# A block-sorted attention with a bilinear feed-forward: one engine-model ordering of all work, Strassen products for three batches, and q and v of two batches by DMA

## The chip, the cores and the metric

The kernel runs on one core of one Trainium2 chip. The metric is the device time of one execution in microseconds (us). Before and after run in turn on the same chip. A profile is taken of one of the runs; its span, from the first to the last instruction, is about 1 to 2 us shorter than the time.

Engines are named as the profile names them: PE (TensorE, matmuls), PEld (its weight loads), DVE (VectorE), ACT (ScalarE), POOL (GpSimd), SP (SyncE, which only issues DMAs here).

## The reference

```python
# q, k, v: (4, 8, 768, 64); sort_net: (4, 8, 8, 8)
P = sort_net
for _ in range(5):                                   # Sinkhorn
    P = exp(P - max(P, -1)); P = P / sum(P, -1); P = P / sum(P, -2)
k_sorted = einsum('bhij,bhjcd->bhicd', P, k_blocks)  # 8 blocks of 96 tokens
v_sorted = einsum('bhij,bhjcd->bhicd', P, v_blocks)
attn = softmax(scale * q_b @ k_sb^T) @ v_sb          # inside each block
x = attn, heads side by side                         # (3072, 512)
out = ((x @ w_a) * (x @ w_b)) @ w_out                # w_a, w_b: 512 x 1536
```

There are four batches of 768 tokens. The feed-forward part has by far the most arithmetic: per batch, the two products with `w_a` and `w_b` ("a, b products") are 48 groups of four matmuls, and the product with `w_out` ("output stage") is six groups of twelve.

## The kernel before

The order of the PE instructions is written by hand: the attention of the next batch is dealt out, unit by unit, between the a, b products of this one.

```python
tc.tile_pool(name="psA", bufs=2, space=PSUM) as psA   # attention: [P, 2, 512] tiles
tc.tile_pool(name="psB", bufs=1, space=PSUM) as psB   # transposes
tc.tile_pool(name="psF", bufs=3, space=PSUM) as psF   # products: [P, 512] tiles, one bank

def ffn_a(b, m, t, pool):
    pf = ffn_mm(b, m, t, w_a_sb, pool)        # four matmuls of 128 x 384 into a psF tile
    a_sb = ffp.tile([P, HW], BF16, tag="a_sb", bufs=4)
    nc.scalar.copy(out=a_sb, in_=pf[:, 0:HW])
def ffn_b(b, m, t, pool):
    pf = ffn_mm(b, m, t, w_b_sb, pool)
    nc.vector.tensor_tensor(out=hT..., in0=a_sb..., in1=pf..., op=ALU.mult)
def ffn_out(b, t, c, pool):
    po = pool.tile([P, DMODEL], FP32, tag="F")
    for m in range(KO):                       # twelve matmuls of 128 x 512
        nc.tensor.matmul(po, lhsT=hT[:, m, c0:c0 + P], rhs=w_out_sb[:, m, :], ...)
    copy(nc.scalar if c % 2 == 0 else nc.vector, o_sb, po)
    ... # two DMA stores
... # (attention: transposes of q and v on PE, mixing of k and v on PE, scores, exp, products, transposes)
```

The softmax here doesn't subtract the row's maximum and nothing guards it: scores larger than these inputs give would overflow.

## Time and profile before

The profile's span is 259.0 us.

First the page: a line with each engine's busy time, the busy tenths of PE and the clock granted to it in 40 slices of the span, and the chain of waits that ended last, by engine and by line.

```profile
PE 247.8 (96%) x2406; PEld 146.9 (57%) x2415; DVE 126.7 (49%) x293; ACT 98.2 (38%) x191; POOL 50.9 (20%) x71
...
PE   6978999999999999999999999999999999999992
...
PEclk9999999999999999999999999999999999999999
...
PE 88%; DVE 2%; POOL 2%; ACT 2%; DMA 2%; issue 1%; POOLq 0%; ACTq 0%
```

PE is busy in every slice after the start, at full clock, and 88% of the chain is PE. So time can only be taken out by taking work off PE, or by shortening the start (first a, b product at 27.25 us).

### The profile page before, as it was taken

What the parts mean: (1) busy time and instruction counts of PE and PEld (TensorE: products, weight loads), DVE (VectorE), ACT (ScalarE), POOL (GpSimd) and SP (SyncE); (2) the same over time, 40 slices, a digit from 0 to 9 for tenths busy, and PEclk for the clock granted to TensorE, in tenths of its full rate; (3) what the DMA queues carried; (4) which work ended last, traced back from release to release, by engine and by line L of the source; (5) the groups of instructions that cost most, each with busy time, mean ns of one, the idle gap of its engine ahead of it and who ended that gap; (6) DMA issues with size and microseconds to landing.
All of it is one profiled execution on the core that took longest, in us unless ns stands there. A gap on an engine that the chain in (4) does not pass through costs nothing.

```text
span 259.0 us, 5786 instructions
## 1 busy us (share of the span) xinstructions
PE 247.8 (96%) x2406; PEld 146.9 (57%) x2415; DVE 126.7 (49%) x293; ACT 98.2 (38%) x191; POOL 50.9 (20%) x71
## 2 busy tenths in 40 slices
PE   6978999999999999999999999999999999999992
PEld 2457566666664466666664466666654466665440
DVE  6676466577771146575751147675651134444110
ACT  3267243355540144634431154545431043333010
POOL 8866369825550000000000000000000000000000
PEclk9999999999999999999999999999999999999999
DMA  5999999999999730110104330110114430000253
GB/s 76 181 202 203 202 201 164 153 191 197 171 195 195 165 83 4 30 33 3 30 6 102 87 84 7 27 33 1 33 19 94 93 70 0 3 0 0 52 114 81
DMA packets 32442, 23.19 MB, mean 90 GB/s; under 512 B 11424, under 2 KB 29344, under 8 KB 32416
## 3 DMA queue, kind: packets, MB, share of 16 engines
q0 software_dynamic: 18928, 14.16, 36.6%
q1 hardware_dynamic: 13488, 8.66, 16.7%
q8 instruction: 19, 0.31, 0.5%
q14 instruction: 7, 0.06, 0.1%
HBM read 28.32 MB, written 6.29 MB: 134 GB/s over the span
## 4 chain that ended last, share of the span: by engine, by line
PE 88%; DVE 2%; POOL 2%; ACT 2%; DMA 2%; issue 1%; POOLq 0%; ACTq 0%
PE pf L255 49%; PE po L282 24%; PE mix L169 4%; PE o_ps L212 3%; PE q_ps L156 3%; PE vs_ps L199 3%; PE sc L187 2%; DMA q_100<-in_q_dram 2%; PE xt_ps L237 1%; DVE xT L144 0%; DVE hT L270 0%; ACT qT L142 0%; ACT kT_106 L142 0%; ACT kT_109 L142 0%; ACT kT_108 L142 0%
## 5 line engine op out<-in xcount | busy, mean ns | idle before, releaser
L255 PE MATMUL pf<-xT,w_a_sb 128*128 128x384 bf16 x384 | 78.2, 326 | 0.4 <-DVE xT L144 0.4
L255 PE MATMUL pf<-xT,w_b_sb 128*128 128x384 bf16 x384 | 78.2, 326 | 0.0
L270 DVE TENSOR_TENSOR hT<-a_sb,pf 128x384 bf16<-128x384 bf16 x96 | 53.0, 552 | 49.7 <-PE pf L255 47.6
L263 ACT CAST a_sb<-pf 128x384 bf16<-128x384 f32 x96 | 45.9, 478 | 78.2 <-DVE hT L270 41.7
L282 PE MATMUL po<-w_out_sb,hT 128*128 128x512 bf16 x280 | 62.4, 379 | 0.4
L255 PEld LDWEIGHTS <-w_a_sb 128*128 128x128 bf16 x384 | 36.0, 98 | 22.8 <-issue 0.6
L255 PEld LDWEIGHTS <-w_b_sb 128*128 128x128 bf16 x384 | 35.8, 98 | 22.3
L282 PEld LDWEIGHTS <-hT 128*128 128x128 bf16 x288 | 28.1, 98 | 33.4
L142 ACT COPY o_sb<-po 128x512 f32<-128x512 f32 x16 | 9.4, 586 | 56.5 <-PE po L282 53.7
L144 DVE COPY o_sb<-po 128x512 f32<-128x512 f32 x8 | 5.5, 691 | 45.5 <-PE po L282 45.5
L218 DVE TENSOR_TENSOR xp<-o_ps,rec 96x512 bf16<-96x512 f32 x32 | 21.4, 683 | 0.4
L309 PE MATMUL w_ps<-warm_sb 128*128 128x512 bf16 (+1 forms) x54 | 11.6, 369 | 2.4 <-DVE warm_sb L303 2.0
L144 DVE COPY qT<-q_ps 128x768 bf16<-128x768 bf16 (+1 forms) x16 | 8.0, 502 | 9.2 <-PE q_ps L156 9.2
L191 ACT ACTIVATE eT_116<-sc 96x768 bf16<-96x768 f32 x12 | 9.3, 808 | 1.0 <-PE sc L187 0.9
L309 PEld LDWEIGHTS <-warm_sb 128*128 128x128 bf16 x55 | 4.9, 108 | 7.5 <-issue 3.4
L216 DVE RECIPROCAL rec<-o_ps 96x8 f32<-96x8 f32 x32 | 5.6, 190 | 5.5 <-PE o_ps L212 5.5
L191 ACT ACTIVATE eT_117<-sc 96x768 bf16<-96x768 f32 x10 | 7.6, 806 | 0.9 <-PE sc L187 0.9
L191 ACT ACTIVATE eT_118<-sc 96x768 bf16<-96x768 f32 x10 | 7.6, 806 | 0.9 <-PE sc L187 0.9
L296 POOL TENSOR_TENSOR s_all<-mask,p_col 128x1024 bf16<-128x1024 bf16 x3 | 5.9, 2008 | 0.0
L201 DVE COPY vs_119<-vs_ps 96x512 bf16<-96x512 bf16 (+1 forms) x8 | 4.4, 549 | 2.8 <-PE vs_ps L199 2.8
L201 DVE COPY vs_120<-vs_ps 96x1024 bf16<-96x1024 bf16 (+1 forms) x6 | 3.5, 588 | 2.7 <-PE vs_ps L199 2.7
L142 ACT CAST kT_106<-mix 128x384 bf16<-128x384 f32 x8 | 3.4, 482 | 3.5 <-PE mix L169 3.5
(230 smaller groups left out, 200.2 us busy)
## 6 DMA issues: line engine op xcount, KB each, us to landing
out_dram<-o_sb SPq DMA_DIRECT2D x48, 128.0 KB, 2.4
w_a_sb<-in_moe_w_a_dram POOLq DMA_DIRECT2D x4, 384.0 KB, 9.0
w_b_sb<-in_moe_w_b_dram POOLq DMA_DIRECT2D x4, 384.0 KB, 9.5
w_out_sb<-in_moe_w_out_dram POOLq DMA_DIRECT2D x3, 512.0 KB, 7.6
q_82<-in_q_dram POOLq DMA_DIRECT2D x2, 96.0 KB, 5.5
k_80<-in_k_dram POOLq DMA_DIRECT2D x1, 192.0 KB, 4.2
v_81<-in_v_dram POOLq DMA_DIRECT2D x1, 192.0 KB, 4.8
q_88<-in_q_dram POOLq DMA_DIRECT2D x2, 96.0 KB, 6.3
```

Of the source, the lines that this page charges most:

```text
L142: nc.scalar.copy(out=out, in_=in_)
L144: eng.tensor_copy(out=out, in_=in_)
L156: nc.tensor.matmul(q_ps[e * D:(e + 1) * D, c, :], lhsT=q2[p0:p0 + np_, e, c * D:(c + 1) * D], rhs=ident[p0:p0 + np_, p0:p0 + np_], is_tran ...
L169: nc.tensor.matmul(mix[e * D:(e + 1) * D, c // 4, c % 4 * P:(c % 4 + 1) * P], lhsT=src2[:, e, c * D:(c + 1) * D], rhs=s_all[:, 2 * g + e], ...
L191: nc.scalar.activation(out=eT[:, h, :, 0:HB], in_=sc[0:BLK, :, 0:HB], func=AF.Exp, scale=float(scale))
L201: nc.vector.tensor_copy(out=vs[:, i0:i0 + n, :, 0:D], in_=vs_ps[0:BLK])
L218: nc.vector.tensor_tensor(out=_ap(xp, h * NBH * 2 * D, [[NB * 2 * D, BLK], [D, 2], [2 * D, NBH], [1, D]]), in0=_ap(o_ps, 0, [[1024, BLK], ...
L255: nc.tensor.matmul(pf[:, 0:HW], lhsT=w_sb[:, kc, m * P:(m + 1) * P], rhs=xTs[b][:, kc, t * HW:(t + 1) * HW], start=(kc == 0), stop=(kc == ...
L263: nc.scalar.copy(out=a_sb, in_=pf[:, 0:HW])
L270: nc.vector.tensor_tensor(out=_ap(hTs[b], m * S + t * HW, [[KO * S, P], [CG, NBH], [NBH * CG, NCH], [1, CG]]), in0=st[b, m, t].rearrange(" ...
L282: nc.tensor.matmul(po, lhsT=hT[:, m, c0:c0 + P], rhs=w_out_sb[:, m, :], start=(m == 0), stop=(m == KO - 1))
L309: nc.tensor.matmul(w_ps[:, 0:cols], lhsT=warm_sb[:, 0:P], rhs=warm_sb[:, 0:cols], start=True, stop=True)
```

## The change

The intent: (1) every piece of work is listed with an engine, an estimated duration, its dependencies, the buffers that it takes and gives back, and a rank; a small model of the engines plays the list through and the kernel issues everything in the order that comes out. (2) The a, b products of batches 1 to 3 use seven block products in place of eight (Strassen's scheme in Winograd's form), 168 matmuls in place of 192 per batch. (3) q of batches 2 and 3 is transposed by DMA; v of those batches is mixed token-major, written to DRAM and read back in the layout that is wanted. Both take transposes off PE. The core of the diff, cut (names: `xT` is the transposed result of the attention, which the products read; `tx` and `ws` are the sums of x blocks and of weight blocks that Strassen's scheme needs; `hT` is the product of a and b, which the output stage reads; `kT` is the mixed k; `vm` is the mixed v, `vd` its copy in DRAM and `vs` what is read back):

```diff
-    psA, psB, psF pools (2 x two banks, 1 bank, 3 x one bank)
+    ps = [psp.tile([P, 2, 512], FP32, name=f"ps{n}") for n in range(4)]   # all of PSUM
+    def buf(key):
+        cls, i = plan.where[key]
+        if cls == "pair": return ps[i]                       # both banks
+        if cls == "bank": return ps[i // 2][:, i % 2, :]     # one bank of a pair
+    class Plan:                     # list scheduler: picks the earliest start, then the rank
+        def _bank(self, cls, now):  # keeps a time for each of the 8 banks, by itself
+            ...
+    QDMA = lambda b, p: b >= 2
+    VDMA = lambda b, p: b >= 2
+    def mix_copy(eng, b, p, what, h, tc_order):
+        st_c, st_t = (1, NCH) if tc_order else (CG, 1)       # NCH is 6
+        copy(ENG[eng], _ap(to, o0, [[2 * HK, P], [st_c, NCH], [BLK, n], [st_t, CG]]),
+             _ap(mix, i0 * CG, [[1024, P], [P, NCH], [CG, n], [1, CG]]))
+    def ab_strassen(b, g, rk, ws_ok, tx_ok, hdeps):          # once for a, once for b
+        p1 -> bank A; copy A (s1); p2 -> bank X; c11 = s1 + X
+        p6 added into A; copy A (u2); p5 -> bank Y
+        p7 added into A; copy A (u3); p4 added into A (c21); c22 = u3 + Y
+        p3 added into Y; c12 = u2 + Y
+    ...                             # sums of weight blocks once, of x blocks per batch
+    if b + 2 < B:
+        for p in range(HP):
+            attention(b + 2, p, RB + 138.0 + 0.5 * p)
+    tx_ok = x_sums(b + 1, RB + 49.0)
+    for g in range(G):
+        ab_strassen(b + 1, g, RB + 50.0 + 4 * g, ws_ok, tx_ok, out_last[b])
+    order = plan.solve()
+    for op in order:
+        if op.fn is not None: op.fn()
```

The rank line for `attention(b + 2, ...)`: 138 comes after all the Strassen chains of the batch before it (ranks 50 to 70) and just ahead of that batch's output groups (rank 140).

## The prediction

> **What bounds the kernel.** TensorE, from 27 us on. The chain of waits shows PE for 88% of the 259.0 us span: a, b products 48.5%, output products 23.8%, attention matmuls about 15%; the granted clock is 1.00 in every window. In order of time the chain is: start-up until the first product at 27.25 us (loads to 13.5 us, then ACT and DVE evacuations one after another); batch 0's products with batch 1's attention to 76.6; output stages of 15.54 us each; batches 1 and 2, 42.2 us each; batch 3, 31.2 us; 4.7 us of tail. Groups of four 128x384 matmuls take 0.65 us, so 0.163 us per matmul. DVE (49% busy) and ACT (38%) have room.
>
> **What the change does.**
> 1. Strassen in batches 1-3: per batch 192 matmuls of 384 columns become 168. 3 x 24 x 0.163 = 11.7 us less PE work.
> 2. q of batches 2-3 by DMA transpose: 0.46 us of PE per pair gone, eight pairs, 3.7 us. v mixed token-major, written to DRAM and read back: the 0.55 us vs transposes gone, 4.4 us, and the mixing costs no more.
> 3. Batch 0's second half moves ahead of the products. It took about 5.6 us among them; the PE order leaves about 1.2 us there. But ACT and DVE bind the start-up, so I expect the first product 3 to 5 us later, about 31 us: net gain 1 to 2 us.
> 4. Added: per Strassen batch 42 ACT copies (0.48 us each) and 42 DVE sums or products of PSUM (0.55 us), with 18 SBUF products, mostly POOL. The profiled durations overlap: two kT casts of 0.48 us take 0.86 us together, as the Trainium skill says of write acknowledgements ("Perfetto Trace Analysis", Optimizing Scalar/DVE Operations). So I estimate per stage of 27.4 us of PE about 17 us ACT and 23 us DVE: 85% of DVE, close to binding but under PE. POOL, from its 2.0 us product of 1024 elements (1.96 ns each), needs about 0.8-0.95 us a product, 12 us a stage.
>
> **Sum.** First product 31; batch 0 31.2 + 10.6 + 1.2 = to 74; output 15.5; two times 27.4 + 6.5 (attention without q, v transposes) + 15.5 = 98.8; batch 3 27.4 + 15.5; tail 4.7: 236 us. Stalls of PE I add: about 1.5 us per Strassen stage (four chains in flight; each matmul-snapshot-matmul round trip needs about 0.76 us, filled by two or three 0.33 us pieces of other chains). Nearly all the removed PE work lies on the critical path.
>
> **Prediction: 240 us** as timed, 234 to 250 eight times in ten. Faster by over 2%: 0.93; within 2%: 0.05; slower: 0.02.
>
> **What would show it.** The Strassen lines: 168 matmuls per stage in 27 to 30 us of chain; PE over 90% busy in those windows; DVE 80-90%. The q and v transposes absent in batches 2-3. Output stages unchanged at 15.5 us. First product at 29-33 us.
>
> **What would make it wrong.** (a) DVE or the snapshot chains bind: Strassen stages of 33 us or more, PE waiting on ACT or DVE. (b) Small packets: q now arrives in 256-byte pieces; the DMA page's Specifications ("DMA: Bandwidth & Descriptors") want at least 512 B for line rate; here software packets averaging about 750 B cost 80 ns each, worked out from the queue table. DMA is already full until 85 us, so batch 2's q and POOL's queue could be late, and POOL's products with it, stalling Strassen's buffers. (c) The v round trip (two DMAs in series; DMA transposes land in 2.9 us here) on the in-order SP queue behind output stores, holding up batch 2's and 3's output matmuls. (d) Start-up later than 33 us.

## More of the kernel before

260.19 us median of four runs beside the changed kernel (260.04 to 267.32).

The timeline of the last output stage (columns: start us, duration us, engine, line, operation, operands, count; in brackets the idle time before it and who ended it):

```profile
239.02 15.27 PE L282 MATMUL po<-w_out_sb,hT 128*128 128x512 bf16 x69
...
241.38 0.58 ACT L142 COPY o_sb<-po 128x512 f32<-128x512 f32 x1 [2.76 <-PE po L282]
...
249.19 0.59 ACT L142 COPY o_sb<-po 128x512 f32<-128x512 f32 x1 [2.05 <-PE po L282]
```

All six output groups are one unbroken row of matmuls on PE (the line counts 69 of the 72: its window begins after the first matmul, and two records are missing from the trace): while ACT or DVE copies one group out of its bank, PE fills another.

The start, on PE:

```profile
12.59 0.36 PE L341 MATMUL pc_ps<-ident,p_rep 32*128 32x32 bf16 x8
...
27.25 0.81 PE L255 MATMUL pf<-xT,w_a_sb 128*128 128x384 bf16 x4 [0.45 <-DVE xT L144]
```

The first of these spreads the finished Sinkhorn matrix over the partitions; all attention waits for it.

PSUM is split into three pools: two buffers of two banks each (`psA`), one bank (`psB`), and three buffers of one bank each (`psF`). Each buffer is a tile of its own.

## The result, and the profile after

332.35 us median (330.86 to 332.94, four runs). Executions over 1.5% slower than the fastest of the same kernel are left out of the means. Ratios in this document are the mean time of one kernel's fast runs over that of the other's fast runs of the same rounds, so not quite the ratio of the medians quoted: here 1.276, with a 95% interval of 1.2722 to 1.2797. The kernel became 72 us slower; the prediction was 20 us faster.

The page of after, the lines that answer to those of before:

```profile
PE 270.5 (82%) x2353; PEld 152.4 (46%) x2353; DVE 154.7 (47%) x354; ACT 144.8 (44%) x249; POOL 96.7 (29%) x119
...
PE   8999888878898787876899498887798578887972
...
PEclk9999999999999999998599959999879969999998
...
PE 31%; ACT 16%; DVE 8%; issue 5%; DMA 1%; ACTq 0%; SPq 0%; DVEq 0%
PE ps L848 15%; PE ps L779 15%; ACT f L788 7%; DVE f L290 3%; ACT kT L236 3%; ACT eT L531 2%; ACT o L236 2%; DVE hT L290 2%; DVE a L290 2%; ACT a L826 1%; DVE xp L556 1%; DMA xT<-xp 1%; PE ps L541 1%; DMA out_dram<-o 1%; PE ps L485 0%
```

No engine is overloaded: DVE and ACT are below half. Yet the chain now passes through ACT and DVE, and PE has holes everywhere. (The profile follows this chain back only to 118.7 us, so its shares add up to about 64% of the span. PE holds about half of what is covered, where before it held 88% of the whole.) This is the picture of engines that wait for one another in turn, not of one that has too much to do. The granted clock falls to 0.5 or 0.6 in three slices, each the one after a slice in which PE is busy for only 0.4 to 0.6.

The last output stage of after, in the timeline:

```profile
305.67 5.34 PE L848 MATMUL ps<-w_out_sb,hT 128*128 128x512 bf16 x24 [0.51 <-DVE hT L290]
...
311.04 0.59 ACT L236 COPY o<-ps 128x512 f32<-128x512 f32 x1 [6.02 <-PE ps L848]
...
311.68 2.75 PE L848 MATMUL ps<-w_out_sb,hT 128*128 128x512 bf16 x12 [0.67 <-ACT o L236]
...
314.47 0.59 ACT L236 COPY o<-ps 128x512 f32<-128x512 f32 x1 [2.84 <-PE ps L848]
...
315.10 2.75 PE L848 MATMUL ps<-w_out_sb,hT 128*128 128x512 bf16 x12 [0.67 <-ACT o L236]
```

Compare it with the same stage before. PE runs two groups (x24), and the copy of the *first* group starts only at 311.04, when the *second* has ended. Then PE stands still for 0.67 us until the copy is over, and so on: one group every 3.42 us (311.68 to 315.10) in place of one every 2.6. The stage has the same matmuls as before and takes 19.1 us in place of 15.7. The six groups take the two banks of one tile in turn (replaying the kernel's plan off the chip gives this), so the next group needs the very bank whose copy was held up. The prediction had named the stage as unchanged, so this stage alone shows that something other than Strassen is at work.

Two groups of instructions by line and shape (busy us and mean ns of one, then idle before and what ended it):

```profile
L236 ACT CAST kT<-ps 128x768 bf16<-128x768 f32 x12 | 24.9, 2104 | 1.5 <-PE ps L469 1.5
...
L848 PE MATMUL ps<-w_out_sb,hT 128*128 128x512 bf16 x288 | 70.0, 398 | 9.7 <-ACT o L236 9.1 <-DVE hT L290 0.5
```

The evacuation of the mixed k takes 2.1 us on average. In the timeline the eight of batches 2 and 3 take about 2.7 us and the four of batch 1 about 0.8.

The start of after, on DVE and on PE:

```profile
5.02 0.21 DVE L399 TENSOR_TENSOR p_nat<-p_nat,rsum 32x64 f32<-32x64 f32 x1
8.55 0.36 DVE L238 COPY qT<-ps 128x384 bf16<-128x384 bf16 x1 [3.32 <-PE ps L453]
8.83 0.25 DVE L401 TENSOR_REDUCE csum<-p_nat 32x8 f32<-32x64 f32 x1
```
```profile
16.84 0.36 PE L415 MATMUL ps<-ident,p_rep 32*128 32x32 bf16 x8
```

In the middle of the second Sinkhorn round DVE stands for 3.3 us in front of a copy of q whose data are still on their way. The next Sinkhorn step, whose input was ready at 5.23 us, is listed behind this copy and runs only at 8.83. Sinkhorn's result reaches PE at 16.84 us in place of 12.59.

The stages, read from the timeline of PE: "ab" from the first to the end of the last a, b product of a batch, "gap" from there to the first product of the next batch (it contains the output stage). us:

| | first product | ab 0 | gap | ab 1 | gap | ab 2 | gap | ab 3 | last ab to end of span |
|---|---|---|---|---|---|---|---|---|---|
| before | 27.25 | 48.8 | 15.9 | 42.3 | 15.4 | 42.3 | 15.4 | 31.4 | 20.2 |
| predicted | 31 | 43 | 15.5 | 33.9 | 15.5 | 33.9 | 15.5 | 27.4 | 20.2 |
| after | 36.60 | 53.9 | 21.1 | 39.3 | 43.5 | 39.4 | 28.3 | 43.0 | 25.5 |

(The 1.5 us of stalls per Strassen stage, which the prediction adds at the end, are not in its row.) Every column is worse than predicted, and even batch 0, which has no Strassen, lost 5 us.

### The profile page after: what moved, and what is told of

Read it like the earlier page. It is cut to its first block, busy times and chain, and to the rows that moved or that the text cites. A ratio compares the mean times of both kernels' runs of the same rounds, so it can differ in the third digit from the quotient of the medians.

```text
span 330.7 us, 5898 instructions
## 1 busy us (share of the span) xinstructions
PE 270.5 (82%) x2353; PEld 152.4 (46%) x2353; DVE 154.7 (47%) x354; ACT 144.8 (44%) x249; POOL 96.7 (29%) x119
## 4 chain that ended last, share of the span: by engine, by line
PE 31%; ACT 16%; DVE 8%; issue 5%; DMA 1%; ACTq 0%; SPq 0%; DVEq 0%
PE ps L848 15%; PE ps L779 15%; ACT f L788 7%; DVE f L290 3%; ACT kT L236 3%; ACT eT L531 2%; ACT o L236 2%; DVE hT L290 2%; DVE a L290 2%; ACT a L826 1%; DVE xp L556 1%; DMA xT<-xp 1%; PE ps L541 1%; DMA out_dram<-o 1%; PE ps L485 0%
## 5 line engine op out<-in xcount | busy, mean ns | idle before, releaser
L290 POOL TENSOR_TENSOR hT<-a,f 128x384 bf16<-128x384 bf16 x38 | 34.7, 918 | 169.0 <-DVE f L290 169.0
L848 PE MATMUL ps<-w_out_sb,hT 128*128 128x512 bf16 x288 | 70.0, 398 | 9.7 <-ACT o L236 9.1
L788 ACT COPY f<-ps 128x384 f32<-128x384 f32 x108 | 49.2, 484 | 47.8 <-PE ps L779 39.6
L290 DVE TENSOR_TENSOR a<-f,ps 128x384 bf16<-128x384 f32 x54 | 29.5, 550 | 27.1 <-ACT f L788 16.5
L290 DVE TENSOR_TENSOR f<-f,ps 128x384 f32<-128x384 f32 x54 | 29.6, 552 | 24.0 <-PE ps L779 13.0
L779 PE MATMUL ps<-tx,ws_a 128*128 128x384 bf16 x108 | 27.1, 343 | 4.0 <-ACT f L788 2.9
L236 ACT CAST kT<-ps 128x768 bf16<-128x768 f32 (+1 forms) x20 | 28.5, 1456 | 3.7 <-PE ps L469 3.6
L531 ACT ACTIVATE eT<-ps 96x768 bf16<-96x768 f32 x32 | 26.1, 841 | 7.6 <-DVE xp L556 4.7
L779 PE MATMUL ps<-xT,w_a_sb 128*128 128x384 bf16 x72 | 18.5, 338 | 6.2 <-DMA xT<-xp 2.9
L697 PE MATMUL ps<-xT,w_b_sb 128*128 128x384 bf16 x96 | 19.5, 325 | 3.1 <-ACT qT L236 1.1
L697 PE MATMUL ps<-xT,w_a_sb 128*128 128x384 bf16 x96 | 19.5, 325 | 2.9 <-DVE hT L290 2.7
L779 PE MATMUL ps<-xT,w_b_sb 128*128 128x384 bf16 x72 | 18.6, 341 | 1.7 <-ACT f L788 1.6
```

What stands on the lines that cost most here:

```text
L236: nc.scalar.copy(out=out, in_=in_)
L290: ENG[eng].tensor_tensor(out=out, in0=in0, in1=in1, op=op)
L531: nc.scalar.activation(out=buf(("eT", b, p))[:, h, :, 0:HB], in_=buf(("sc", b, p, h))[0:BLK, :, 0:HB], func=AF.Exp, scale=float(scale))
L697: nc.tensor.matmul(pf[:, 0:HW], lhsT=w_sb[:, kc, m * P:(m + 1) * P], rhs=buf(("xT", b))[:, kc, t * HW:(t + 1) * HW], start=(kc == 0), stop ...
L779: nc.tensor.matmul(buf(key)[:, 0:HW], lhsT=lf(j), rhs=rf(j), start=start and j == 0, stop=j == 1, skip_group_check=not start)
L788: return add("ACT", 0.48, lambda: nc.scalar.copy(out=buf((name, b, g, n)), in_=buf(kA)[:, 0:HW]), [dep], get=[("f", (name, b, g, n))], rank=r)
```

## Experiments

Theory A, from the two output stages above: the four PSUM tiles of the change are two banks each, and single-bank work uses one half. Whatever records the program and places the semaphore waits orders accesses by *tile*, so work in one bank is made to wait for work in the tile's other bank. The engine model does not know of it: it keeps eight times, one for each bank. Rivals: B, the strided copies of k (2.7 us in place of 0.8) and what queues behind them on ACT; C, the DMA route for q and v is late; D, the Strassen chains themselves are too tight. The first four runs separate A, B and C, and e1 bears on D too. (The recorded texts use letters of their own: "Rival B" in e1's is D here, "Theory C" in e5's is the placement of the attention, and "Theory D" in e6's is about the start.)

### e1: eight one-bank tiles, same order

```diff
-ps = [psp.tile([P, 2, 512], FP32, name=f"ps{n}") for n in range(4)]
+pb = [psp.tile([P, 512], FP32, name=f"pb{n}") for n in range(8)]
-        if cls == "pair": return ps[i]
-        if cls == "bank": return ps[i // 2][:, i % 2, :]
+        if cls == "pair": return pb[2 * i:2 * i + 2]
+        if cls == "bank": return pb[i]
 # and the operations that span both banks (exp, reciprocal, evacuations) become two, one per bank
```

> The changed kernel with its eight PSUM banks as eight tiles in place of four two-bank tiles; same order of instructions; what reads or writes both banks of a pair is split in two (32 more exponentials, 18 more kT and vT copies, some 70 more DVE instructions). Theory A (the recording layer orders accesses by whole PSUM tile: 127 of the 283 waits of TensorE that name ACT or DVE as producer of a PSUM conflict point at the other bank of the pair): output stages back from 19.6 to 15.6 us, Strassen stages from 39 to 28-31 us, batch 0's products from 55 to 45-48 us; in all 275 to 290 us. Rival B (the snapshot round trips themselves are too slow for four chains): Strassen stages stay at 36 us or more, only the output stages recover; in all 310 us or more.

(The count of waits in this text was made from the built program; no run shows it.)

Measured: correct, 275.91 us (274.75 to 276.89); the kernel before on the same chip 260.95; ratio 1.0547 (1.0475 to 1.0618). That is 56 us of the 72. The last output stage is again one row, in the timeline of e1:

```profile
256.63 12.68 PE L853 MATMUL pb<-w_out_sb,hT 128*128 128x512 bf16 x57
...
258.98 0.59 ACT L236 COPY o<-pb 128x512 f32<-128x512 f32 x1 [2.00 <-PE pb L853]
...
261.57 0.59 ACT L236 COPY o<-pb 128x512 f32<-128x512 f32 x1 [2.00 <-PE pb L853]
```

The copies come every 2.6 us while PE runs on. The result is still correct, so the waits that went were not needed. The Trainium skill ("PSUM — Partial Sum Buffer", PSUM bank collisions raise a hardware error) gives the unit that must be guarded: bank by quadrant of partitions, "by bank is the simple version". By that rule accesses of different banks by different engines may overlap, and this run agrees: its copies out of one bank run while PE fills another, and the outputs are right. The stage times fell everywhere: ab 0 from 53.9 to 44.8, ab 1 from 39.3 to 28.3, ab 2 from 39.4 to 30.0, ab 3 from 43.0 to 33.1. Only ab 3 lies above the range expected; e5 below shows why. The Strassen chains themselves (rival D) are then not what made 39 to 43 us. What two instructions in place of one for each pair operation cost was not measured apart.

### e2: only the order of the k evacuation's loops

```diff
 if tc_order:
-    copy(..., _ap(to, o0, [[2 * HK, P], [1, NCH], [BLK, n], [NCH, CG]]), ...)      # writes in steps of 12 bytes
+    copy(..., _ap(to, o0, [[2 * HK, P], [BLK, n], [NCH, CG], [1, NCH]]), ...)      # writes in order, reads strided
```

> The changed kernel, with the kT copies of batches 2-3 walking their tile in the order of the destination (destination runs of 6 contiguous bf16, source stepping 128 floats in PSUM) in place of a destination step of 6 elements. Same values. Theory A2 (the 12-byte step of the destination makes these ACT copies 2.6 us in place of 0.8, and they hold the scores of batches 2 and 3): copies near 0.8-1.0 us, the stretch from the end of Strassen 1 to the start of Strassen 2 shorter by 8 to 14 us, 318 to 325 us in all. Rival: the stretch is held by q or v that arrive late by DMA, or the cost is in the PSUM side as much: copies or stretch unchanged, 330 us or more.

Measured: 326.65 us (325.54 to 331.56), ratio 1.2474 (1.238 to 1.2568), so about 6 us less than after. The group of the copies in e2:

```profile
L236 ACT CAST kT<-ps 128x768 bf16<-128x768 f32 x12 | 9.6, 808 | 1.5 <-PE ps L469 1.5
```

The mechanism was right (2104 to 808 ns on average, 15.3 us of ACT gone), the size was overestimated: only about 6 of the 15 lay on the path, and the stretch from ab 1 to ab 2 became only 2.5 us shorter (43.5 to 41.0), not 8 to 14. (After was timed in another job than e2; e3 against e1, in one job, gives 6.3 us for the same edit.) The Trainium skill's "SBUF — State Buffer" (Door 1: The DMA port swizzle) notes 16-byte lines in SBUF and that each access crossing to a new line pays a penalty. It agrees in direction: the destination step was 6 bf16, 12 bytes, so three elements of four began a new line, and the same copy with 2-byte steps took under a third of the time. The run shows the cost of the step, not the lines themselves. That the step of the reads from PSUM became 512 bytes instead did no visible harm.

### e3: both

The edits of e1 and e2 together.

> Both edits together. If A and A2 are the whole of the loss: 255 to 270 us, below or near the kernel before; output stages 15.6 us, Strassen 28-31 us, granted clock 1.00 throughout. If a third cause exists (late DMA of q or v, in-order queues, the start-up at 36.6 us), 275 us or more.

Measured: 269.63 us (267.78 to 270.49), ratio 1.0299 (1.0224 to 1.0374). The two edits are nearly independent (the second is worth about 6 us alone and 6.3 on top of the first), and 9 us above before remain, while Strassen should have put the kernel below it. So there is a third cause. The stage table of e3 points to it: its ab stages are 44.8, 28.3, 28.7 and 32.6 us, but the gap from ab 1 to ab 2 is 37.6 us and from ab 2 to ab 3 23.8 us, with 15.4 before. The chain of waits of e3 in the first of them (start us, us, what):

```profile
128.07 7.37 DMA vd<-vm
...
136.17 0.58 PE pb L857
...
159.47 4.17 DMA xT<-xp
...
164.76 1.31 PE pb L788 x7
```

The write of v to DRAM and, later, the transposing DMA to xT stand on the chain themselves. What waits for the write is DVE's copy of the third v pair, because there are two `vm` buffers; the first output group stands 5.15 us behind that copy on PE. The reading is that nothing covers these transfers, because all four pairs of a later batch's attention were placed at the end of the stage.

### e4: e1 with q and v of batches 2 and 3 on PE again

```diff
-QDMA = lambda b, p: b >= 2
-VDMA = lambda b, p: b >= 2
+QDMA = lambda b, p: False
+VDMA = lambda b, p: False
```

This also brings the k copies back to their contiguous order, so it is to be compared with e3.

> Single-bank tiles, and q and v of batches 2-3 back on TensorE transposes (kT in plain order too, so no strided copy), the rest (Strassen, the listed order) kept. If the DMA route for q and v is worth what I predicted once the rest is repaired: 4 to 8 us slower than e3. If it costs: faster than e3. Strassen stages 28-31 us under A.

Measured: 264.13 us (263.22 to 265.42), ratio 1.0101 (1.0018 to 1.0184), 5.5 us below e3. In this order of work the DMA route, which takes about 8 us of transposes off PE, costs time. The reading at this point is that its latency is exposed, not that it is bad in itself; the next runs test that.

### e5: e3 with the attention of batches 2 and 3 beside the products

```diff
-            attention(b + 2, p, RB + 138.0 + 0.5 * p)
+            attention(b + 2, p, RB + 52 + 8 * p)
```

> e3 with one edit: the attention of batches 2 and 3 is ranked beside the products of the batch two before it (one pair every 8 units of rank from the start of that Strassen stage) and not at the stage's end. Theory C (the attention of batches 2 and 3 is listed so late that its latencies, with one xT buffer, stand at the stage boundaries): the gaps from the last product of a Strassen stage to the first of the next fall from 37.6 and 23.8 us to about 22 and 18, the Strassen stages grow by a few us each as they take up the attention matmuls, total 252 to 262. Rival: the gaps are the xT round trip itself (last out group, transposing DMA, x sums) and stay above 30 and 22; total within 3 us of e3's 269.6.

Measured: 251.97 us (250.66 to 252.16), with 260.35 for the kernel before on this chip; ratio 0.9645 (0.9584 to 0.9706). One rank moved the kernel from 3% above before to 3.5% below it. The gaps are 18.8 and 17.5 us, ab 1 and ab 2 took up the attention and are 34.9 and 32.8 us, and ab 3 is 28.1, because it no longer waits for xT (2.60 us of that DMA and 1.04 us of x sums stood inside e3's ab 3). The two `vm` buffers were kept, so it was the placement and not their number. The chain of e5 through the same output stage:

```profile
134.61 5.29 PE pb L857 x24
...
143.51 7.77 PE pb L857 x36
151.29 2.92 PE pb L788 x18
```

It is PE from end to end.

### e6: e5 with a repaired start

```diff
-        qd = q_part(0, p, 0, rk)
+        qd = q_part(0, p, 0, rk, [sink[3] if p == 0 else reps[1] if p == 1 else o_pc])
-            n = int((o.start - t - 0.05) / 0.056)          # warm-up matmuls that fill PE
+            n = int((o.start - t - 0.05) * 0.6 / 0.056)
```

(`sink[3]` is the end of the fourth Sinkhorn round, `o_pc` the matmuls that spread its result.)

> e5 with a second edit: the first q transposes of batch 0 wait in the list until the Sinkhorn rounds are nearly done (q0 after the fourth, q1 after the spread of p, q2 and q3 after the matmuls that spread it over the partitions) and the warm-up matmuls are cut to 0.6 of their number. Theory D (Sinkhorn's DVE chain stands in line behind a q copy, and the matmuls that spread p behind warm-ups): the matmuls that spread p fall from 17.0 to about 13 us, the first product from 35.6 to 30 to 33, total 2.5 to 6 us below e5. Rival: the start is bound by the loads of k, v and the weights: the first product stays at 35 or later and the total within 1 us of e5.

Measured: 249.69 us (248.47 to 250.89), ratio 0.9557 (0.9478 to 0.9637) in the same job. This is the best version: 4.4% below the kernel before and, by the medians, 25% below the change. The page of e6:

```profile
PE 236.6 (95%) x2229; PEld 141.2 (57%) x2229; DVE 151.4 (61%) x420; ACT 133.5 (54%) x312; POOL 104.0 (42%) x126
...
PE   7986999999999999989999999999999999999992
```

PE is busy throughout again. But theory D (of the start) was only half right. Sinkhorn's result now reaches PE at 11.81 us, earlier than in before, yet the first product came only one step forward, from 36.1 to 34.6 us. Two lines of e6's timeline suggest why that was not enough:

```profile
11.81 0.46 PE L416 MATMUL pb<-ident,p_rep 32*128 32x32 bf16 x8 [0.51 <-DVE p_rep L238]
...
20.57 0.38 PE L454 MATMUL pb<-ident,q 64*64 64x64 bf16 x12 [1.94 <-DMA q<-in_q_dram]
```

PE soon stands in line again, now for the second halves of batch 0's q (e10 to e12 below ask whether that holds the start), and the difference between e6 and e5, 2.3 us, lies close to the spread of the runs.

### e7: the kernel before, with its three product banks made one tile

The reverse test of theory A, in the kernel that never had the change.

```diff
-tc.tile_pool(name="psF", bufs=3, space=PSUM) as psF          # three tiles of one bank
+tc.tile_pool(name="psF", bufs=1, space=PSUM) as psF
+three = psF.tile([P, 3, 512], FP32, name="three")            # one tile of three banks
+# pf and po take three[:, n % 3, :] in turn, as they took the three buffers
```

> The kernel before with one edit: the three one-bank buffers of the products and of the output matmuls are made the three banks of a single PSUM tile, taken in turn as before. Same instructions in the same order, same banks' worth of space. Theory A (accesses of different banks of one tile are put in order one after the other): every product waits for the evacuation of the product before it, 0.48 to 0.55 us, and every output group 0.6 us: out stages from 15.7 to about 19 us, product stages from 31.4 to 55 or more, total 320 to 375 us. Rival (the loss in e1's undoing had to do with the order or the clock and not with tiles): within 3% of 260.

Measured in one look: correct, 403.83 us (one run, so its state is unknown; the clock is 1.0). The same instructions in the same order, on the same amount of PSUM, took 55% longer than the kernel before. Even the top of the expected range was too low: the first three ab stages are 72 us and the output stages 20.2. The timeline of e7, in a product stage and in the last output stage:

```profile
251.23 0.48 ACT L263 CAST a_sb<-three 128x384 bf16<-128x384 f32 x1 [2.42 <-PE three L255]
251.76 0.81 PE L255 MATMUL three<-xT,w_b_sb 128*128 128x384 bf16 x4 [0.57 <-ACT a_sb L263]
...
386.88 0.59 ACT L142 COPY o_sb<-three 128x512 f32<-128x512 f32 x1 [6.43 <-PE three L282]
387.52 2.75 PE L282 MATMUL three<-w_out_sb,hT 128*128 128x512 bf16 x12 [0.67 <-ACT o_sb L142]
```

The last pair has the same idle time as after's output stage to the hundredth of a microsecond: 0.67 us of PE behind an ACT copy. Here the three banks are taken in turn, so the copy is out of another bank than the one that PE fills next. (In after it was the copy that had waited for the other bank.) With e1 this settles theory A: a tile of several banks makes the wait, and it does so in either kernel.

### e8: e6 without Strassen

```diff
-        tx_ok = x_sums(b + 1, RB + 49.0)
-        for g in range(G):
-            ab_strassen(b + 1, g, RB + 50.0 + 4 * g, ws_ok, tx_ok, out_last[b])
+        for t in range(2):
+            for m in range(KO):
+                ab_plain(b + 1, t, m, RB + 50.0 + (t * KO + m), out_last[b])
```
(and the sums of the weights are left out)

> e6 with the Strassen chains, the weight sums and the x sums of batches 1 to 3 taken out and plain products in their place. If Strassen saves what its matmuls say (168 in place of 192 of 0.163 us, 3.9 us per stage, 11.7 in all) and its chains, sums and waits cost nothing, e8 is 11 to 12 us above e6. If the waits at its start and inside its chains eat it, e8 is within 3 us of e6 or below it. My guess: 3 to 7 us above e6.

Measured: 258.59 us (257.7 to 260.34), ratio 0.9918 (0.9846 to 0.999) to before in the same job as e6. So Strassen is worth 8.9 us of the 11.7 that its matmuls promise. In the last product stage, which has no attention in it, it is 31.6 us against 28.0 with Strassen, 3.6 of 3.9. My guess of 3 to 7 had been too timid.

### e9: e6 with q and v on PE

The edit of e4 on e6.

> e6 with q and v of batches 2 and 3 on TensorE transposes again, everything else as e6. It asks whether the DMA route pays once the attention stands beside the products. If the transposes that the route removes from PE are worth their PE time (about 0.5 us each for q and v of 8 pairs, 8 us in all), e9 is 5 to 9 us above e6. If the route's latencies still eat it, as in e4 against e3 (5.5 us the other way), e9 is equal to e6 or below it. My guess: 4 to 8 us above.

Measured: 260.35 us (258.79 to 261.02), ratio 0.9974 (0.9931 to 1.0017). This was another chip than e6's, so I compare the ratios: 0.9974 against 0.9557, some 4% of 260 us or about 11 us, give or take 2 by the two intervals (the two profiled spans differ by 9.8). The DMA route that cost 5.5 us in e3's order saves about 11 us in this one, more than the 5 to 9 expected. The same edit changed its sign with the placement of its latency.

### e10, e11, e12: what holds the first product at 34.6 us

e10 loads the second halves of batch 0's q ahead of the first weight block in place of behind it:

```diff
-    load_ab(0)
     for p in range(HP):
         q_in[0, p, 1] = load(lambda p=p: q_half(0, p, 1), ...)
+    load_ab(0)
```

> e6 with the second halves of batch 0's q loaded ahead of the first weight block in place of behind it. In e6 the first product is still at 34.6 us and PE stands 1.94 us for such a half at 20.6 us. If that in-order wait is what holds the start, PE's wait for q goes and the first product falls to 30 to 33 us, the total 1.5 to 4 us below e6. Rival: the start is bound elsewhere (the chains of exp, sums and copies between PE's pieces, or the weights that now land later): the first product stays within 1 us of 34.6 and the total within 1.5 us of e6.

Measured: 255.34 us (255.06 to 256.06), ratio 0.9797 (0.9776 to 0.9819): slower than e6 (by ratios, as this is another chip), with the first product at 39.7 us. So the edit gained nothing, but it is no clean test of the idea. PE's last wait for a q half does end 4 us earlier than in e6 (18.07 in place of 22.13 us), but two other things in its trace differ. The granted clock is 0.64 from 12 to 20 us and 0.72 from 20 to 28, where e6 has 1.00 and 0.79. And PE stands 2.07 us at 36.9 us behind a DVE sum of two weight blocks that takes 2.67 us beside one on POOL, which is what e11 shows next.

e11 holds the second halves of q of pairs 1 to 3 back until all first halves have reached xT:

```diff
-        qd = q_part(0, p, 1, rk)
+        qd = q_part(0, p, 1, rk, xT_done[0, 0] if p else [])
```

> e6 with one edit: the second half of batch 0's q (pairs 1 to 3) may be transposed only after all first halves have reached xT, so that PE does not stand in line for those loads. Theory D2 (what holds the first product at 34.6 us in e6 are batch 0's second halves, put ahead of the products by the list: their q lands at about 20.5 us and the in-order PE waits for it): the first product falls to 28 to 32 us, batch 0's products grow by 2 to 4 us as they take the halves back, total 1 to 4 us below e6. Rival: the first product stays at 34 us or later and the total within 1 us of e6, or above it.

Measured: 255.62 us (254.95 to 256.84), ratio 0.9818 (0.978 to 0.9857), first product at 37.2 us, later and not earlier. This does not refute theory D2 by itself: pair 0's second half is exempt from the edit and still holds PE for 1.21 us, and something new costs more than the edit could gain. Its timelines of DVE, of POOL and of PE show it:

```profile
29.39 4.21 DVE L290 TENSOR_TENSOR ws_a<-w_a_sb 128x768 bf16<-128x768 bf16 x1
33.51 0.24 DVE L560 RECIPROCAL rec<-pb 96x4 f32<-96x4 f32 x2
...
34.12 0.74 DVE L566 TENSOR_TENSOR xp<-pb,rec 96x256 bf16<-96x256 f32 x2
```
```profile
29.18 1.66 POOL L290 TENSOR_TENSOR ws_a<-w_a_sb 128x768 bf16<-128x768 bf16 x1
...
31.52 1.65 POOL L290 TENSOR_TENSOR ws_b<-w_b_sb 128x768 bf16<-128x768 bf16 x1
```
```profile
34.92 0.34 PE L574 MATMUL pb<-ident,xp 96*128 96x96 bf16 x4 [3.63 <-DVE xp L566]
```

A sum of two weight blocks, 0.55 us on DVE when alone, is shown with 4.21 us here, from just after POOL began such a sum until POOL's next sum was over. The attention's last steps stand behind it, and PE stands 3.63 us behind them. "SBUF — State Buffer" (SBUF: two separate sides) says that DVE and GpSimd share a pair of ports, that a DVE operation with two SBUF inputs against a GpSimd operation reading SBUF needs it, and that "the other fully blocks". The traces agree in the main: the sum has two SBUF inputs on both engines. In after a DVE sum that began inside a POOL sum took 1.99 us and ended 0.42 us after it. In e6 two such DVE sums ran their usual 0.54 us while POOL's took 2.81 in place of 1.63, and the next one on DVE took 1.49. That the block in e11 lasted over both POOL sums, though POOL has none from 30.84 to 31.52 us, is not explained by one such lock.

e12 adds to e11 that the weight sums too wait until all first halves have reached xT:

```diff
-                d = [w_in[n, c], w_in[n, c + 2]]
+                d = [w_in[n, c], w_in[n, c + 2]] + xT_done[0, 0]
```

> e11 with a second edit: the sums of the weight blocks too wait until all first halves have reached xT. In e6 six such sums of 0.5 to 1.5 us stand on DVE between 29.8 and 39.3 us among the copies that the first products wait for. Theory D3 (these sums hold the first products): the first product another 1 to 3 us earlier than in e11, total 0.5 to 2 us below it. Rival: they only filled idle DVE time: within 0.5 us of e11.

Measured: 250.56 us (249.15 to 251.25), ratio 0.9608 (0.957 to 0.9646), first product at 34.2 us: 3 us earlier than in e11, and 5 us less in all, more than expected. So the sums did hold e11 up. (The recorded text counts six such sums in e6; its timeline has ten from 29.8 to 39.3 us.) But e12 is no better than e6 (ratio 0.9557 on another chip, intervals overlapping). What keeps the first product 7 us behind that of before stays open. The candidates are PE's wait for late q, still 1.86 us in e12 (pair 0's half), the longer row of small steps, and the granted clock, which none of these edits set out to test. From 12 to 28 us the clock is 1.00 in before and e5; it is 0.79 in half of that stretch in e6 and e11 and in all of it in e12, after the warm-up matmuls were cut. It is not the whole, because e5, at 1.00, has its first product at 36.1 us. None of these runs separates the candidates.

## Why the prediction was wrong

**What was read rightly.** PE bound the kernel before, and less PE work does make it faster: e6 is that. The engine loads estimated for a Strassen stage were about right. In e6's last product stage (200 to 228 us in the table by windows) DVE is busy 22.9 us, ACT 19.2, POOL 11.8; predicted were 23, 17 and 12. The stage takes 28.0 us, inside the predicted 27 to 30. Neither DVE nor the snapshot chains bind. So warning (a) came true in its symptom (stages of 39 to 43 us, PE waiting on ACT and DVE) and not in its cause. Warning (b), the small packets, is not what cost the time: with the same packets the route gains in e6.

**The step that failed** is two phrases of the sum: "Output stages unchanged at 15.5 us" and "Stalls of PE I add: about 1.5 us per Strassen stage". Both take it for granted that banks are independent, as they were in the kernel before. In after they are not: the waits are placed by tile. The sum should have held a term for waits between the two banks of a tile. It measured 56 us (after against e1), in every stage: about 9 us in batch 0's products, 9 to 11 in each Strassen stage, 3.3 in the first output stage. I had costed every operation that the diff adds and removes and had passed over the line that changes no operation, the declaration of the PSUM tiles.

**Second, a latency placed where nothing covers it.** The prediction let batches 1 and 2 take "6.5 (attention ...)" in a stage and 15.5 for the output, as if the attention were dealt out between the products as before. The rank of 138 puts it at the boundary. This measured 17.7 us by the medians of e3 and e5 (17.0 by their ratios, as they ran on two chips). The prediction's own warning (c), the v round trip holding up output matmuls, came true in part: 7.37 us of the write stand on e3's chain in front of batch 1's first output group. But no output store stood before it on SP, as the warning had it; the few `vm` buffers and the late placement did it.

**Third, the k copies.** The prediction has no term for them; its "the mixing costs no more" speaks of v. The copy's step of 12 bytes made it 2.7 us in place of 0.8; this measured about 6 us of time.

**Fourth, the start.** Predicted 31 us, with a warning at 33; measured 36.6. Whether "ACT and DVE bind the start-up" was right is not shown: in after DVE stood 3.3 us behind a q copy, in e6 PE behind q loads. Of the total, e6 took back 2.3 us; the rest is open.

**The sizes of the two gains.** Strassen: 11.7 us predicted, 8.9 measured (e8 against e6). The DMA route: 8.1 us predicted, 10 to 11 saved in e6's order, 5.5 lost in e3's.

By medians the steps are: 332.4, less 56.4 (tiles), 6.3 (copies), 17.7 (placement), 2.3 (start), which is 249.7. Each step starts from the one before, so the sum is no check of its own. The last two runs come from another chip, on which the kernel before was 0.6 us faster. The prediction's sum of 236 us is still 12 us under e6's span of 248.4: 3.6 for the first product, 5 for the gaps after ab 1 and ab 2 (18.8 and 17.4 us in place of 15.5, with pieces of attention among the output groups), the rest in small amounts in the other columns.

## What to carry to other kernels

When a change re-declares buffers, ask for each tile which accesses the recording layer will put in order, and compare that unit with the unit of the scheduler's own model; here a tile that was wider than the unit of work cost a wait per use. Look first at a stage that the change should not touch: here the output stage, with the same matmuls and a new idle time of about 0.7 us before each group from the third on, pointed to the cause, which e1 and e7 then showed. And a route that takes work off the busiest engine by adding latency pays only where other work covers the latency; the same route cost 5.5 us in one order and saved 10 to 11 in the other.

## What the Trainium skill lacked or had wrong

- "PSUM — Partial Sum Buffer": the rule by bank agrees with e1 (quadrants were not tested), but nothing says that the program as recorded may be ordered more coarsely, by whole tile. Three banks in one tile took the kernel before from 260 to 404 us (e7), and four two-bank tiles cost 56 us (e1).
- "SBUF — State Buffer": the note on 16-byte lines has no figure for a write by ACT. A 128x768 copy from PSUM to bf16 took about 2.7 us with a destination step of 12 bytes and 0.81 us with steps of 2 bytes (after, e2).
- "SBUF — State Buffer": the exclusive lock of the ports that DVE and GpSimd share has no example of two sums on both engines. A 0.55 us sum on DVE was shown with 4.21 us beside two of 1.65 us on POOL (e11).
- "DMA: Bandwidth & Descriptors": beyond its fit for a single DMA I found no figure for a round trip from SBUF to DRAM and back. In the chain of e6 the write of a v pair takes 4.2 to 4.3 us and the read 2.6 to 2.8 us; on e3's chain the write stands with 7.4 us.
